# First six chunks decayed singly and converted weights placed late, in a kernel ordered by a planner

## The chip, the cores and the metric

The kernel runs on one core of a Trainium2 chip. The metric is device time in microseconds (us) of one execution. TensorE (PE) does the matrix products and transposes, VectorE (DVE), ScalarE (ACT) and GpSimd (POOL) the rest, and SyncE (SP) issues all transfers between DRAM and SBUF; each engine takes its own instructions strictly in order, and waits on semaphores for the others.

## The reference, cut to what matters

Linear attention with a decay per feature, then a soft mixture of eight experts over all tokens, then a gated layer. All data are float32; 4 batches of 768 tokens, 8 heads of 48.

```python
for t in range(S):
    state = alpha[:, :, t, :, None] * state + k_t v_t^T
    y[:, :, t] = q_t @ state
# y as x: 3072 tokens x 384
logits = x @ phi                      # 32 slots
slots = softmax over tokens(logits).T @ x
slots = relu(slots @ w1) @ w2         # per expert, 4 slots each
x = softmax over slots(logits) @ slots
out = (silu(xn @ w_gate) * (xn @ w_val)) @ w_out    # xn: x by its root mean square
```

## The kernel before

The 24 chunks of 128 tokens (6 per batch) go through attention one after the other. For chunk n the program has named operations. `sc n` makes the scores on PE (16 matmuls, line 509), `sb n` copies them out on ACT (L513), `sm n` sets the upper triangle to zero on POOL (L517). `kn n` turns the keys on PE (L496). `iv n` multiplies the scores with the values and the keys with the values (L530, L535), and `o n` adds what the old state gives (L543, L547). `sv n` writes the new state on DVE (L553), and `o n+1` waits for it. `x n` turns the result to token rows (L560). For a first chunk of a batch there is no old state, and `o n` stands for `iv n`.

Scores need decayed keys and queries. They are prepared for a *unit* of chunks at once (`units_of`): unit 0 is chunk 0, unit 1 chunks 1 and 2, and every further one three chunks. A unit of more than one chunk comes in two groups, two head pairs each, and a chunk can be scored only after both. For group x, `R x` is the running product of the decays (two scans on DVE, L449), `I x` its inverse (L457 and two scans, L458), `k x` the product of keys and inverse on DVE (L473), and `q x` that of queries and `R x` on POOL (L473 too; `BY_POOL` names the units for which POOL does it, here all nine). Rows come by SP (L431): decays into a ring of 2 places, keys and queries into rings of 5 places each. A place is taken again only after its last reader.

After every four chunks a softmax group follows (`gl`, `g1`, `gt`, `gd`, `s1`, `ga`, `s3`), and at the end `join` (`m1` to `mi`, where `siT` is made) starts the experts: `h` is the hidden layer (L749), `ht` its transpose (L760), `r` the second product (L770), eight of each; `sT` picks the slots. The expert weights are 64 loads of 384 KB (`w 1 ..`, `w 2 ..`; L734, L736), issued by SP all along the attention, each into one of 58 blocks of SBUF (`Q`). The gated layer then makes gates (`pg`, L902), and for each of 6 groups of 4 chunks and 12 slices of the feed-forward width the products `gv` (L1019), `sg`, `mu` (DVE, L1056), `hh`, `hl` (DVE, L1061) and `mm` (L1026 to L1028).

The weights of the gated layer arrive as 64-bit numbers and are converted in five steps (`wide_ops`): `cl` loads a piece (384 KB; L382), `ca` splits it on ACT (L385, L386), `cb` clamps on DVE (L389, L390), `cc` adds on POOL (L394), and `cd` writes the result on DVE (L397). `cl` takes the block of the raw numbers and also the block that `cd` will write into; `ca` takes a third one for its parts. 15 pieces (`g` for gate and value, `o` for the output weights) are loaded before the gated layer.

Nothing of the order is written by hand. Every operation is given to a `Plan` with an engine, an estimated cost, a priority, its predecessors and the places it takes and frees. `Plan.times` plays this through once when the program is built: at each step it takes, over all engines, the operation that could start first, but an engine may leave out one that is ready for one of lower priority number that becomes ready soon (`SOON`, `WAIT`, `LONG`, `LATE`, `CRIT`). The sequence that results is the order in which instructions are issued. Warm-up transposes (`wu`, L1089, four each, number `WARM`) have the last priority: they stand where PE had, by the plan, nothing else.

Of the kernel before, what the change touches and what calls it, by code (L numbers as in the profile page):

```python
# [16 lines left out]
P = 128  # L17
# [6 lines left out]
class Plan:  # L24
# [57 lines left out]
    def times(self):  # L82
# [29 lines left out]
        while ready:  # L112
# [24 lines left out]
            for e, b in best.items():  # L137
                x = min(b)
                wait = SOON if x[1] < LATE else WAIT if x[1] < CRIT else LONG
                c.append(min((y for y in b if y is x or y[0] <= x[0] + wait and y[1] < CRIT), key=lambda y: (y[1], y[2])) if wait else x)  # L140
# [36 lines left out]
BY_POOL = [("q", u) for u in range(9)]  # L177
WARM = 6
# [8 lines left out]
OHOLD = ("hl", 0, 0)  # L187
# [3 lines left out]
LD, KD_, SD_ = 0.8, 1.4, 1.4  # L191
XD, GD, CK = 3.366, 1.917, -7.005
AHEAD, BACK = 4, 4
EX0, EX_AT, EX_BY = 1, 4, 0.4
XA, XB, XC, GB1 = 195.8, 197.2, 197.4, 0.5
# [23 lines left out]
def network(tc, q, k, v, al, phi, w1, w2, wg, wv, wo, rg, aP, kP, qP, vP, phP, out):  # L219
# [33 lines left out]
    V.tensor_tensor(fold[:, 0, :], ident[:, 0:32], ident[:, 32:64], ALU.add)  # L253
    V.tensor_tensor(fold[:, 0, :], fold[:, 0, :], ident[:, 64:96], ALU.add)
    V.tensor_tensor(fold[:, 0, :], fold[:, 0, :], ident[:, 96:128], ALU.add)
    for g in range(1, 4):
        V.tensor_copy(fold[:, g, :], fold[:, 0, :])
# [113 lines left out]
    def wide_ops(plan, key, dst, w, prio, after, hold, new, use):  # L371
# [29 lines left out]
        plan.op(nm("cl"), "SP", 1130, prio[0], load, after, new=[cv, lim, *new], use=use)  # L401
# [260 lines left out]
    def join(plan, prio):  # L662
# [17 lines left out]
        plan.op("m1", "PE", 110, prio, lambda: T.transpose(plan("kn", "m1")[0:1, 0:P], m0, ident), [("g1", g)], new=[("kn", "m1")])  # L680
# [28 lines left out]
    def experts(plan, after, prio, n0=None):  # L709
# [142 lines left out]
    def gated(plan, prio):  # L852
# [25 lines left out]
        for i, key in enumerate(rest):  # L878
# [9 lines left out]
            w = ("Q", ("wf", f))  # L888
# [197 lines left out]

    def warm(bank, n):
# [11 lines left out]
    for u, (c0, j, groups) in enumerate(units):  # L1099
        for g, (p0, n) in enumerate(groups):  # L1100
            x, w = (u, g), n * j * C
            t = c0 - j + j * g / len(groups) - LD if u else -10
            for i, nm in enumerate("akq"):
                plan.op(("l", nm, x), "SP", 1.45 * w, t - 2 + 0.1 * i, lambda nm=nm, x=x: load_nat(nm, *x), last.get(nm, []), new=[(RING[nm], x)])
# [4 lines left out]
            for nm in "kq":  # L1109
                e, en, cost = (G, "Pool", 2.6 * w) if (nm, u) in BY_POOL else (V, "DVE", 60 + 1.3 * w)  # L1110
# [5 lines left out]
    for n in range(NCH):  # L1116
# [173 lines left out]
```

## Time and profile before

| | us |
|---|---|
| three runs, median (lowest to highest) | 405.32 (400.57 to 405.67) |
| the profiled execution | 403.42 |
| its span, from the first to the last instruction | 401.6 |
| PE, DVE, ACT, POOL busy in the span | 374.9, 299.0, 216.8, 122.6 |
| last chunk's product with the state (`o 23`) begins | 144.17 |
| first matmul of the experts | 152.15 |
| last pieces of the experts' second product (`r 1 3`) | 179.08 to 182.2 |
| first `mm` of the gated layer | 194.63 |
| last addition of the result on DVE | 394.75 |

The execution is 1.8 us longer than its span. The 1.9 us between it and the median are less than the spread of the three runs.

### The profile page before, as it was taken

How to read it: one execution, taken by the hardware profiler on the slowest of the kernel's cores; microseconds unless marked ns; L12 is line 12 of the kernel's file. 1: busy time of each engine (PE TensorE's matmuls, PEld its weight loads, DVE VectorE, ACT ScalarE, POOL GpSimd, SP SyncE). 2: the span in 40 equal slices, each digit the busy share in tenths (PEclk: the TensorE clock that was granted, in tenths of full speed). 3: DMA queues.
4: the chain of work that ended last, by engine and by line, in shares of the span. 5: the costliest groups of instructions: out<-in, count | busy, mean ns of one | idle time of the engine just before them, and what ended most of it. 6: DMA issues, size and time to landing. Idle time of an engine off the chain costs nothing.

```text
span 401.6 us, 8927 instructions
## 1 busy us (share of the span) xinstructions
PE 374.9 (93%) x3427; PEld 316.1 (79%) x3427; DVE 299.0 (74%) x563; ACT 216.8 (54%) x469; POOL 122.6 (31%) x150
## 2 busy tenths in 40 slices
PE   7689979998899999999889999999999999999993
PEld 6578858785777865436578999979899999999992
DVE  7999979879898557615989987769855667657652
ACT  2336535666574847311676786858856444444440
POOL 3445452635665415600155523243400000000000
PEclk9769989999999999999969999999999999999997
DMA  7899998996989679993021323213000102102012
GB/s 270 282 330 316 333 347 297 341 373 255 341 266 341 204 229 342 346 325 113 2 78 43 116 78 114 85 41 118 0 2 0 53 27 81 55 24 81 32 48 87
DMA packets 29252, 68.43 MB, mean 170 GB/s; under 512 B 3600, under 2 KB 9872, under 8 KB 29200
## 3 DMA queue, kind: packets, MB, share of 16 engines
q1 hardware_dynamic: 29200, 67.77, 48.7%
q8 instruction: 29, 0.48, 0.5%
q14 instruction: 23, 0.19, 0.1%
HBM read 63.04 MB, written 4.72 MB: 169 GB/s over the span
## 4 chain that ended last, share of the span: by engine, by line
PE 64%; DVE 16%; DMA 12%; issue 3%; ACT 2%; POOL 1%; SPq 0%; DVEq 0%; POOLq 0%; ACTq 0%
PE pstr L1019 4%; PE pssc L1019 4%; PE psmisc L1026 3%; PE pskn L1028 3%; PE psmisc L1028 3%; PE psy L1026 3%; PE psmisc L1027 3%; PE psU L1026 3%; PE pssc L509 3%; PE psy L1028 3%; PE psy L1027 3%; PE psU L1028 3%; PE psU L1027 3%; PE pskn L1026 3%; PE psy L530 3%
## 5 line engine op out<-in xcount | busy, mean ns | idle before, releaser
L1061 DVE TENSOR_TENSOR b<-b,b 128x512 fp32r<-128x512 f32 (+1 forms) x73 | 50.7, 697 | 26.3 <-PE psmisc L1027 10.1
L394 POOL TENSOR_TENSOR b<-b 128x384 int32<-128x384 int32 x36 | 40.5, 1126 | 96.5 <-DVE b L390 40.4
L1058 ACT CAST b<-b 128x512 fp32r<-128x512 f32 (+1 forms) x73 | 44.8, 617 | 36.6 <-DVE b L1056 34.5
L1056 DVE TENSOR_TENSOR b<-b,pssc 128x512 f32<-128x512 f32 (+1 forms) x73 | 49.2, 677 | 15.4 <-ACT b L1054 15.0
L1054 ACT ACTIVATE b<-pstr 128x512 f32<-128x512 f32 (+1 forms) x73 | 43.0, 594 | 24.2 <-PE pstr L1019 21.8
L517 POOL TENSOR_SCALAR_AFFINE_SELECT b<-b 128x512 f32<-128x512 f32 x48 | 32.2, 690 | 35.0 <-ACT b L513 34.9
L473 POOL TENSOR_TENSOR b<-b,b 128x768 f32<-128x768 f32 (+1 forms) x17 | 28.9, 1705 | 26.6 <-DVE pstr L457 12.2
L530 PE MATMUL psy<-b,b 128*48 128x128 f32 x384 | 29.7, 295 | 5.2 <-POOL b L517 4.3
L513 ACT COPY b<-pssc 128x512 f32<-128x512 f32 x48 | 26.7, 592 | 12.6 <-PE pssc L509 12.5
L458 DVE TENSOR_TENSOR_SCAN b<-b,pstr 128x387 f32<-128x387 f32 (+1 forms) x34 | 31.0, 912 | 1.7
L449 DVE TENSOR_TENSOR_SCAN b<-b,pstr 128x387 f32<-128x387 f32 (+1 forms) x34 | 29.0, 894 | 3.5 <-DMA b<-in_alpha_rows_dram 3.5
L509 PE MATMUL pssc<-b,b 48*128 48x128 f32 x384 | 30.1, 294 | 1.6 <-ACT b L513 1.2
L397 DVE SCALAR_TENSOR_TENSOR b<-b,b 128x384 int32<-128x384 int32 x36 | 27.2, 764 | 5.8 <-POOL b L394 5.8
L1019 PE MATMUL pssc<-y,b 128*128 128x512 f32 (+1 forms) x73 | 29.3, 401 | 2.1 <-DVE b L1056 1.7
L509 PEld LDWEIGHTS pssc<-b,b 48*128 48x128 f32 x384 | 24.8, 194 | 7.6 <-issue 4.9
L530 PEld LDWEIGHTS psy<-b,b 128*48 128x48 f32 x384 | 22.3, 131 | 10.5 <-POOL b L517 5.2
L1019 PE MATMUL pstr<-y,b 128*128 128x512 f32 (+1 forms) x73 | 29.4, 403 | 0.4 <-DVE b L906 0.4
L385 ACT ACTIVATE b<-b 128x384 f32<-128x384 f32 x36 | 20.8, 577 | 11.6 <-DMA b<-in_moe_w_val_dram 4.1
L1026 PE MATMUL pskn<-b,b 128*128 128x384 f32 x72 | 25.5, 354 | 0.2 <-ACT b L1058 0.2
L1028 PE MATMUL pskn<-b,b 128*128 128x384 f32 x72 | 24.9, 345 | 0.8 <-DVE b L1061 0.8
L1026 PE MATMUL psmisc<-b,b 128*128 128x384 f32 x72 | 24.7, 343 | 0.1
L1026 PE MATMUL psU<-b,b 128*128 128x384 f32 x72 | 24.6, 341 | 0.1
(226 smaller groups left out, 884.0 us busy)
## 6 DMA issues: line engine op xcount, KB each, us to landing
b<-in_moe_w_dram SPq DMA_DIRECT2D x64, 384.0 KB, 5.8
b<-in_alpha_rows_dram SPq DMA_DIRECT2D x14, 387.5 KB, 5.6
b<-in_k_rows_dram SPq DMA_DIRECT2D x14, 384.0 KB, 5.0
b<-in_q_rows_dram SPq DMA_DIRECT2D x14, 384.0 KB, 5.6
b<-in_v_rows_dram SPq DMA_DIRECT2D x24, 192.0 KB, 5.2
b<-in_moe_w_gate_dram SPq DMA_DIRECT2D x12, 384.0 KB, 4.8
b<-in_moe_w_val_dram SPq DMA_DIRECT2D x12, 384.0 KB, 3.9
b<-in_moe_w_out_dram SPq DMA_DIRECT2D x12, 384.0 KB, 3.8
```

Source lines behind the costliest of these rows:

```text
L394: G.tensor_tensor(ui, ui, r(), ALU.add)
L509: T.matmul(heads(plan(*sc_of(n)[a]))[:, p, :], kq("Tk", n, p)[r], kq("Tq", n, p)[r], start=True, stop=True)
L517: G.affine_select(s, s, pattern=[[0, NP], [1, C]], compare_op=ALU.is_ge, fill=0.0, base=0, channel_multiplier=-1)
L530: T.matmul(y[64 * a:64 * a + D, p, :], vv[:, h], heads(plan("scS", (n, a)))[:, p, :], start=p == 0, stop=first and p == NP - 1)
L1019: T.matmul(plan(r, ("gv", j, f))[:, s], G4(f // 3, a)[:, f % 3 * P:(f % 3 + 1) * P], plan("c4a", j)[:, s].bitcast(F32R), start=True, stop= ...
L1026: T.matmul(po, h, wo_of(f)[:, 0, :], start=(f % HALF == 0), stop=False)
L1027: T.matmul(po, h, wo_of(f)[:, 1, :], start=False, stop=False)
L1028: T.matmul(po, l, wo_of(f)[:, 0, :], start=False, stop=(f % HALF == HALF - 1))
L1054: plan.op(part("sg"), "ACT", 176 + 416 / np, pg, lambda g=g, SG=SG, s=s: A.activation(SG()[:, s], plan(*g)[:, s], AF.Silu), [part("gv"), * ...
L1056: plan.op(part("mu"), "DVE", 130 + 546 / np, pg, lambda val=val, SG=SG, s=s: V.tensor_tensor(SG()[:, s], SG()[:, s], plan(*val)[:, s], ALU ...
L1058: plan.op(part("hh"), "ACT", 194 + 422 / np, pg, lambda SG=SG, HH=HH, s=s: A.copy(HH()[:, s], SG()[:, s]), [part("mu"), *pre("hh")], new=n ...
L1061: lambda SG=SG, HH=HH, HL=HL, s=s: V.tensor_tensor(HL()[:, s], SG()[:, s], HH()[:, s], ALU.subtract), [part("hh"), *pre("hl")], new=new(hl),
```

## The change

There are nine edits in one.

1. `units_of`: the first six chunks are units of their own, with all four head pairs in one group. `BY_POOL` is widened to all units of the new count.
2. The priority of `sv n` is n - 1 in place of n, that of the rows and decays of the single chunks is set by `U1`, `U2`.
3. The matrix `fold`, the sum of four blocks of the identity, is made by POOL as an operation `fo` after `sm 4`, and not by DVE at the start.
4. `WARM` is 26 in place of 6.
5. `cl` no longer takes the block that is written into: for `g` pieces `cd` takes it, for `o` pieces `cd` writes into the block of the parts.
6. The pieces `o 3` to `o 5` may be converted once `sT 1` is done (`OHOLD`), before that after the first `hl`.
7. The second part of the root mean square (`sq`, `rm` to `rs`) has a later priority (`XB`, `XC`).
8. Expert weights are spread further in priority (`EX_BY`).
9. An engine may wait for a more urgent operation at least as long as the one ready would take; some estimated costs are changed.

```diff
-                wait = SOON if x[1] < LATE else WAIT if x[1] < CRIT else LONG
+                wait = SOON if x[1] < LATE else WAIT if x[1] < CRIT else max(LONG, ops[x[3]][1])
...
-BY_POOL = [("q", u) for u in range(9)]
-WARM = 6
+BY_POOL = [("q", u) for u in range(24)]
+WARM = 26
...
-OHOLD = ("hl", 0, 0)
+OHOLD = ("sT", 1)
...
+U1, U2, SV = -3, 0.8, 1
+SINGLE = 6
...
-EX0, EX_AT, EX_BY = 1, 4, 0.4
-XA, XB, XC, GB1 = 195.8, 197.2, 197.4, 0.5
+EX0, EX_AT, EX_BY = 1, 4, 0.6
+XA, XB, XC, GB1 = 195.8, 198.2, 199.4, 0.5
...
-    u = [(0, 1), (1, 2), (3, 3)] + [(c, 3) for c in range(6, chunks, 3)]
+    u = [(c, 1) for c in range(SINGLE)] + [(c, 3) for c in range(SINGLE, chunks, 3)]
...
-    V.tensor_tensor(fold[:, 0, :], ident[:, 0:32], ident[:, 32:64], ALU.add)
-    V.tensor_tensor(fold[:, 0, :], fold[:, 0, :], ident[:, 64:96], ALU.add)
-    V.tensor_tensor(fold[:, 0, :], fold[:, 0, :], ident[:, 96:128], ALU.add)
-    for g in range(1, 4):
-        V.tensor_copy(fold[:, g, :], fold[:, 0, :])
...
-        plan.op(nm("cl"), "SP", 1130, prio[0], load, after, new=[cv, lim, *new], use=use)
+        plan.op(nm("cl"), "SP", 1190, prio[0], load, after, new=[cv, lim])
...
-        plan.op(nm("cd"), "DVE", 650, prio[1], sign, [nm("cc")], use=[cv, cx, lim, *new, *use])
+        first = [("cd", (*key[:3], 0))] if key[0] == "g" and key[3] else []
+        plan.op(nm("cd"), "DVE", 650, prio[1], sign, [nm("cc"), *first], new=new, use=[cv, cx, lim, *use])
+    wf_of = lambda f: ("Q", ("cx", ("o", f)) if wide else ("wf", f))
...
+    def folds():
+        for i in range(1, 4):
+            G.tensor_tensor(fold[:, 0, :], fold[:, 0, :] if i > 1 else ident[:, 0:32], ident[:, 32 * i:32 * i + 32], ALU.add)
+        G.tensor_copy(fold[:, 1:4, :], fold[:, 0:1, :].to_broadcast([P, 3, NS]))
...
-            t = c0 - j + j * g / len(groups) - LD if u else -10
+            t = -10 if not u else U1 + U2 * u if j == 1 else c0 - j + j * g / len(groups) - LD
...
-            plan.op(("sv", n), "DVE", 350, n, lambda n=n: state(n), [("o", n), *[("ck", (u, g)) for g in gs]], use=[("U", n), ("gm", u)])
+            plan.op(("sv", n), "DVE", 350, n - SV, lambda n=n: state(n), [("o", n), *[("ck", (u, g)) for g in gs]], use=[("U", n), ("gm", u)])
...
+    plan.op("fo", "Pool", 900, AHEAD, folds, [("sm", AHEAD, 1)])
```

What it does to the order is seen at three places. The first is PE at the start, up to what follows the scores of chunk 0 (`pskn` holds turned keys, `pssc` scores, `psy` the result of a chunk, `psmisc` is the bank of the warm-up transposes). Before:

```order
L1089 MATMUL psmisc_70<-ident 128x128 x24
L496 MATMUL pskn_67<-ident,b_97 128x128 x4
L509 MATMUL pssc_65<-b_102,b_97 128x128
L509 MATMUL pssc_66<-b_102,b_97 128x128
...
L530 MATMUL psy_69<-b_114,b_118 48x128
L530 MATMUL psy_69<-b_115,b_118 48x128
...
L535 MATMUL psU_68<-b_118 48x48 x8
L496 MATMUL pskn_67<-ident,b_98 128x128 x2
```

The same place in the changed kernel, up to the scores of chunk 1:

```order
L1095 MATMUL psmisc_70<-ident 128x128 x28
L497 MATMUL pskn_67<-ident,b_91 128x128 x4
L510 MATMUL pssc_65<-b_96,b_91 128x128
L510 MATMUL pssc_66<-b_96,b_91 128x128
...
L1095 MATMUL psmisc_70<-ident 128x128 x20
L497 MATMUL pskn_67<-ident,b_92 128x128 x4
L510 MATMUL pssc_65<-b_97,b_92 128x128
L510 MATMUL pssc_66<-b_97,b_92 128x128
```

All 24 warm-up transposes stood at the very start; now 28 stand there, 20 between the scores of chunk 0 and the keys of chunk 1 (whose scores now come ahead of chunk 0's product with the values), 4 before the scores of chunk 2, 8 between `o 3` and `iv 4`, 16 around `join` and before `r 1 3`, and 28 behind the last `mm`.

The second place is DVE from the keys of the second group on (`b_98`, `b_99`, `b_100` are keys, `psU` the sum for the state). Before:

```order
L473 TENSOR_TENSOR b_98<-b_98,b_113 128x512
L253 TENSOR_TENSOR fold<-ident 128x32
L254 TENSOR_TENSOR fold<-fold,ident 128x32
L255 TENSOR_TENSOR fold<-fold,ident 128x32
L257 COPY fold<-fold 128x32 x3
L449 SCALAR_TENSOR_TENSOR b_111<-b_107,pstr_63 128x258 x2
...
L473 TENSOR_TENSOR b_99<-b_99,b_112 128x512
L449 SCALAR_TENSOR_TENSOR b_109<-b_108,pstr_63 128x387 x2
...
L473 TENSOR_TENSOR b_100<-b_100,b_113 128x768
L553 TENSOR_TENSOR b_115<-psU_68,b_114 128x192
```

The same stretch of the changed kernel (`b_92` to `b_94` are the keys of chunks 1 to 3):

```order
L474 TENSOR_TENSOR b_92<-b_92,b_107 128x512
L450 SCALAR_TENSOR_TENSOR b_105<-b_101,pstr_63 128x258 x2
...
L474 TENSOR_TENSOR b_93<-b_93,b_106 128x512
L554 TENSOR_TENSOR b_109<-psU_68,b_108 128x192
L450 SCALAR_TENSOR_TENSOR b_103<-b_102,pstr_63 128x258 x2
...
L474 TENSOR_TENSOR b_94<-b_94,b_107 128x512
L450 SCALAR_TENSOR_TENSOR b_104<-b_102,pstr_63 128x258 x2
L554 TENSOR_TENSOR b_108<-psU_68,b_108 128x192
```

The six instructions of `fold` are gone, each key product now completes a chunk, and the first state step (`sv 0`) stands behind the keys of chunk 2, where those of chunks 1 and 2 and a half of 3 to 5 stood ahead of it.

The third place is DVE at the start of the gated layer, from the last `hl` of the first slice to that of the second one (`cN` and `ss` belong to the root mean square; L389, L390 and L397 before are L386, L387 and L394 after). Before:

```order
L1061 TENSOR_TENSOR b_2374<-b_2360,b_2371 128x256
L990 SCALAR_TENSOR_TENSOR cN<-cN,rr 128x640
L906 TENSOR_TENSOR b_2357<-pstr_64,b_2357 64x384
L389 TENSOR_SCALAR b_2390<-b_2390 128x384
L390 TENSOR_SCALAR b_2390<-b_2390 128x384
L906 TENSOR_TENSOR b_2357<-pssc_65,b_2357 64x384
L389 TENSOR_SCALAR b_2400<-b_2400 128x384
L390 TENSOR_SCALAR b_2400<-b_2400 128x384
L397 SCALAR_TENSOR_TENSOR b_2257<-b_2256,b_2390 128x384
L1056 TENSOR_TENSOR b_2409<-b_2409,pssc_66 128x512
L397 SCALAR_TENSOR_TENSOR b_2261<-b_2260,b_2400 128x384
L1061 TENSOR_TENSOR b_2436<-b_2409,b_2428 128x512
```

The same stretch of the changed kernel:

```order
L1062 TENSOR_TENSOR b_2442<-b_2426,b_2437 128x256
L965 TENSOR_TENSOR b_2428<-psmisc_70,cN 128x128
L1057 TENSOR_TENSOR b_2452<-b_2452,pssc_66 128x512
L892 TENSOR_TENSOR b_2462<-b_2366,b_2462 128x384
L907 TENSOR_TENSOR b_2431<-pssc_65,b_2431 64x384
L1062 TENSOR_TENSOR b_2472<-b_2452,b_2469 128x512
```

Ten instructions between the two became four; the conversions of `o 3` and `o 4` moved ahead of the first `hl`, and the root mean square from there to behind the second one.

## Rows read from the trace of the kernel before

**Rows 1.** Busy us of each engine in a stretch; then PEclk, DMA share, GB/s.

```profile
10.00:20.00 10.00, 6.86 (x58) 5.33 (x58) 9.45 (x22) 3.07 (x10) 4.79 (x5) 0.72 0.83 282
```

**Rows 2.** Stretches of 4 us, with the same columns.

```profile
96.00:100.00 4.00, 2.77 (x35) 1.66 (x32) 3.90 (x9) 3.15 (x8) 1.65 (x3) 1.00 0.42 122
160.00:164.00 4.00, 4.00 (x58) 1.68 (x54) 3.46 (x7) 1.32 (x3) 2.65 (x3) 1.00 1.00 359
```

**Rows 3.** Tile `ident` up to 10 us: ns of one, minimum, median, maximum.

```profile
L1089 PEld LDWEIGHTS psmisc<-ident x24: 183/230/230, 1.5 to 6.3; 128*128 128x128 f32 x24
...
L496 PEld LDWEIGHTS pskn<-ident,b x4: 140/142/143, 7.9 to 8.2; 128*128 128x128 f32 x4
```

**Rows 4.** Timeline of PE: start, duration, instruction, idle time before it and its end.

```profile
21.47 2.07 PE L509 MATMUL pssc<-b,b 48*128 48x128 f32 x14 [1.24 <-ACT b L513]
...
33.71 1.16 PE L509 MATMUL pssc<-b,b 48*128 48x128 f32 x16
...
38.09 1.16 PE L509 MATMUL pssc<-b,b 48*128 48x128 f32 x16
...
55.93 1.73 PE L530 MATMUL psy<-b,b 128*48 128x128 f32 x13 [2.59 <-POOL b L517]
...
60.94 1.16 PE L509 MATMUL pssc<-b,b 48*128 48x128 f32 x16
...
125.40 0.71 PE L509 MATMUL pssc<-b,b 48*128 48x128 f32 x8
```

**Rows 5.** Timeline of DVE in attention; the last row is a stretch of the softmax tile.

```profile
7.80 1.26 DVE L449 TENSOR_TENSOR_SCAN b<-b,pstr 128x258 f32<-128x258 f32 x2
...
11.47 0.61 DVE L253 TENSOR_TENSOR fold<-ident 128x32 f32<-128x32 f32 x1
...
12.84 1.27 DVE L449 TENSOR_TENSOR_SCAN b<-b,pstr 128x258 f32<-128x258 f32 x2
...
27.30 1.79 DVE L449 TENSOR_TENSOR_SCAN b<-b,pstr 128x387 f32<-128x387 f32 x2
...
32.76 1.80 DVE L449 TENSOR_TENSOR_SCAN b<-b,pstr 128x387 f32<-128x387 f32 x2
...
48.00 0.95 DVE L473 TENSOR_TENSOR b<-b,b 128x768 f32<-128x768 f32 x1
...
60.03 0.36 DVE L553 TENSOR_TENSOR b<-psU,b 128x192 f32<-128x192 f32 x1 [2.71 <-PE psU L547]
...
122.84 0.95 DVE L473 TENSOR_TENSOR b<-b,b 128x768 f32<-128x768 f32 x1
...
47.00:57.00 10.00, 1.29 (x10) 0.36 (x10) 2.18 (x9) 1.30 (x5) 0.92 1.02 378
```

**Rows 6.** Timelines of SP and POOL: a load of queries and its product.

```profile
46.76 0.80 SPq L431 DMA_DIRECT2D b<-in_q_rows_dram  x2
...
53.65 1.63 POOL L473 TENSOR_TENSOR b<-b,b 128x768 f32<-128x768 f32 x1 [3.73 <-DVE pstr L457]
```

**Rows 7.** Timeline of PE from the last chunk to the end of the experts.

```profile
144.17 1.08 PE L543 MATMUL psy<-b,b 48*48 48x128 f32 x16
...
152.15 2.80 PE L749 MATMUL pssc<-b,siT 128*32 128x256 f32 x48 [0.35 <-DVE siT L692]
...
167.76 1.47 PE L770 MATMUL pskn<-b,x 128*32 128x384 f32 x16
...
179.08 3.14 PE L770 MATMUL pskn<-b,x 128*32 128x384 f32 x16
...
182.15 0.87 PE L1089 MATMUL psy<-ident 128*128 128x128 f32 x6
```

**Rows 8.** Timeline of DVE at the start of the gated layer, and its last addition.

```profile
196.29 0.82 DVE L990 SCALAR_TENSOR_TENSOR cN<-cN,rr 128x640 f32<-128x640 f32 x1
...
202.96 0.68 DVE L1061 TENSOR_TENSOR b<-b,b 128x512 fp32r<-128x512 f32 x1
...
209.88 0.68 DVE L1061 TENSOR_TENSOR b<-b,b 128x512 fp32r<-128x512 f32 x1
...
394.75 0.56 DVE L1077 TENSOR_TENSOR b<-psmisc,b 128x384 f32<-128x384 f32 x1
```

More of the change, by code (lines that the diff above doesn't have):

```diff
@@ L412, in piece @@
         else:
-            t, w, m, at = ("Q", ("wf", key[1])), wo[key[1] * P:(key[1] + 1) * P], 0, 0
+            t, w, m, at = wf_of(key[1]), wo[key[1] * P:(key[1] + 1) * P], 0, 0
         dst = lambda: plan(*t)[:, at:at + CW]
-        new, use = ([], [t]) if m else ([t], [])
+        new, use = ([], [t]) if m else ([] if wide and key[0] == "o" else [t], [])
         if wide:
@@ L678, in m9 @@
                 T.matmul(plan("kn", "m9")[:, kk * NS:(kk + 1) * NS], acc[:, kk * P:(kk + 1) * P], foldS, start=True, stop=True)
-        plan.op("m1", "PE", 110, prio, lambda: T.transpose(plan("kn", "m1")[0:1, 0:P], m0, ident), [("g1", g)], new=[("kn", "m1")])
+        plan.op("m1", "PE", 110, prio, lambda: T.transpose(plan("kn", "m1")[0:1, 0:P], m0, ident), [("g1", g), *[x for x in ["fo"] if x in plan.ops]], new=[("kn", "m1")])
         plan.op("m2", "DVE", 450, prio, m2, ["m1"], use=[("kn", "m1")])
@@ L739, in experts @@
         for i, x in enumerate(seq):
-            plan.op(("w", *x), "SP", 1130, EX_AT + i * EX_BY, lambda x=x: load(*x), [("w", *seq[i - 1])] if i else after,
+            plan.op(("w", *x), "SP", 1190, EX_AT + i * EX_BY, lambda x=x: load(*x), [("w", *seq[i - 1])] if i else after,
                     new=[("Q", (f"w{x[0]}", *x[1:]))])
@@ L887, in gated @@
                 continue
-            w = ("Q", ("wf", f))
+            w = wf_of(f)
             plan.op(("hi", f), "ACT", 510, po, lambda f=f, w=w: A.copy(wo_of(f)[:, 0, :], plan(*w)[:, 0:DM]), [("cd", key), *(["mi"] if f else [])], new=[("Q", ("wo", f))], use=[w])
@@ L1101, in network @@
             x, w = (u, g), n * j * C
-            t = c0 - j + j * g / len(groups) - LD if u else -10
+            t = -10 if not u else U1 + U2 * u if j == 1 else c0 - j + j * g / len(groups) - LD
             for i, nm in enumerate("akq"):
-                plan.op(("l", nm, x), "SP", 1.45 * w, t - 2 + 0.1 * i, lambda nm=nm, x=x: load_nat(nm, *x), last.get(nm, []), new=[(RING[nm], x)])
+                plan.op(("l", nm, x), "SP", 1.52 * w, t - 2 + 0.1 * i, lambda nm=nm, x=x: load_nat(nm, *x), last.get(nm, []), new=[(RING[nm], x)])
                 last[nm] = [("l", nm, x)]
@@ L1109, in network @@
             for nm in "kq":
-                e, en, cost = (G, "Pool", 2.6 * w) if (nm, u) in BY_POOL else (V, "DVE", 60 + 1.3 * w)
+                e, en, cost = (G, "Pool", 2.35 * w) if (nm, u) in BY_POOL else (V, "DVE", 60 + 1.45 * w)
                 plan.op((nm, x), en, cost, t, lambda nm=nm, x=x, e=e: prep_m(nm, *x, e), [("l", nm, x), ("R" if nm == "q" else "I", x)],
```

## Prediction

> **What bounds the kernel now.** I read the stretches first, then the timelines of PE and DVE side by side. The time table gives PE 374.9 of 401.6 us, 93%, so whatever shortens the run must close gaps or slow stretches of PE. There are three places with such loss. At the start DVE works without a pause and PE waits for it: in 10 to 20 us DVE is busy 9.45 of 10, PE 6.86, at a granted clock of 0.72 [rows 1], and 14 score matmuls take 2.07 us at 21.5, where 16 take 1.16 at 33.7 [rows 4], that is 148 ns each against 72: the lower of the two clock levels, 1.2 GHz in place of 2.4. In the experts DMA ends the waits: the last product, 16 matmuls, lasts 3.14 us where its kind needs 1.47 [rows 7]. At the start of the gated layer DVE again: the second `mm` needs an `hl` that DVE begins only at 202.96 [rows 8], 8.3 us after the first `mm`. I take the rest, the other 70 slices, to cost the same in either kernel.
>
> **The start, part by part.** DVE first. A group of 512 columns (two scans, the inverse, the keys) lasts 11.47 - 7.80 = 3.67 us, and `fold` 12.84 - 11.47 = 1.37 [rows 5]. A group of 768 lasts 32.76 - 27.30 = 5.46, of which one state step is 0.26, so 5.2 [rows 5]. Six chunks singly cost 6 x 3.67 = 22.0, plus 0.5 where the first key product runs beside POOL; in units of 1, 2 and 3 chunks they cost 3 x 3.67 + 2 x 5.2 = 21.4. So single chunks cost DVE 0.6 us and `fold` gives back 1.4; the keys of chunk 5 come at 3.7 + 22.5 + two state steps and a wait of about 0.5, some 27.3, as before (27.3, the start of the next group [rows 5]). DVE gains next to nothing. What changes is PE: chunk 1 can be scored at 11.5 and not after both groups of unit 1 (12.84 + 3.67 = 16.5), chunk 3 at 3.66 + 4 x 3.67 + 0.5 + 0.3 = 19.1 and not at 27.3, where PE had to begin three chunks at once.
>
> PE needs 38.09 - 33.71 = 4.4 us per chunk at the full clock [rows 4], DVE 4.0 with the state step, so PE trails DVE by one chunk through the first six. I walked both queues. `o 0` ends near 15.8 (20 transposes of 0.145 us stand ahead of it: six last 0.87 [rows 7]), while DVE reaches `sv 0` at 15.3: it stands 0.5 to 0.7 there, and with it `R 3` and all decays behind. `sv 1` to `sv 4` find their products done. Two groups more of 5.2 with three state steps put chunks 6 to 8 at 38.9, hardly later than before (32.76 + 5.46 = 38.2), and two more, now with the first softmax on DVE as well (2.2 us here, the softmax tile's row [rows 5]), put chunk 9 at about 53.4, 1.9 us of it for state steps, waits and products slowed beside POOL. PE has finished `kn 8` by 50.4 and begins `sc 9` at 53.4. Before, it began at 60.94 [rows 4], though its keys were ready at 48.95 [rows 5]: POOL stood 3.73 us at the queries of a later group, with `sm 7` queued behind them, because these were loaded only at 46.76, when chunk 5 had given its place in the ring free [rows 6]; PE then waited 2.59 for POOL [rows 4], and DVE 2.71 for PE's state [rows 5]. With one place per single chunk the same queries wait for chunk 4, which by the same walk ends 11 us sooner. **The gain at chunk 9 is 60.94 - 53.4 = 7.5 us.**
>
> That it lasts to the end of attention is not given. At PE's own pace `o 23` begins at 144.17 - 7.5 [rows 7]. DVE must bring the keys of the last unit in time. Before, from the keys of chunk 9 (48.95) to those (122.84 + 0.95 = 123.8) it took 74.8 us [rows 5]. The changed order has in this stretch two conversions less (three instructions of 384 columns; by the 0.68 of 512 columns [rows 8] 0.5 each, 3.0 in all) and a softmax group less (2.2); the stop of 2.71 for PE's state [rows 5] falls away, since PE is then ahead. That leaves 66.9, and 53.4 + 66.9 = 120.3. PE began these scores at 125.40 [rows 4], and wants them at 117.9: 2.4 lost if DVE had no other wait in the 66.9, nothing if it had 2.4 of waits on PE, which come earlier with PE. I take 0.5.
>
> **Transposes and clock.** The 28 at the start end near 7.9, when the first keys come, so they cost nothing. The 20 fill a gap ahead of chunk 1 in which PE stood idle. Row by row: while PE did nothing but 24 transposes, its weight loads took 230 ns; right behind them, with no other matmul in between, they took 142 [rows 3]. So here transposes alone raised it. The Trainium skill ("TensorE: Matmul & The Clock Gate", Part 4: PE-mode transpose) says that transposes don't count as work in this way and don't bring the full clock. Rows 3 speak against that; what would follow from it is rival B. The 16 around `join` cost 0 in its waits and 8 x 0.145 = 1.2 ahead of `r 1 3` if its weights are there. The 28 at the end can start once the last addition is done, at 394.75 + 0.56 = 395.3 [rows 8]; 28 x 0.145 are 4.1, and the span goes on to 401.6, 6.3 later, for the output's transfer, so 0, at most 1; I take 0.2.
>
> **`fold` on POOL** has no row: DVE did it in 1.37, and where DVE needs 0.95 for 768 columns POOL needs 1.63 [rows 5, 6]; at that ratio 2.4. But POOL does it in four instructions and not six, so 1 to 2.4; I take 1.5. Behind it queue the queries of unit 6 and `sm 5`; both wait for DVE or PE beyond that, so 0, and 1.5 at the other bound, for `iv 5` alone.
>
> **Blocks and DMA.** The `cl` pieces took two blocks per `g` pair and one per `o` more. When these ran out, SP stood with all rows behind it: in 96 to 100 DMA moved 122 GB/s, against 359 when fed [rows 2]. By the order, SP now meets its first block to wait for only when all keys are issued. Behind the first expert layer's first product 19 loads are left, where there were 21; one load of 0.393 MB at 359 GB/s is 1.1 us, so the DMA-bound end comes 2.2 nearer to `mi`. DMA must, however, keep up with a PE that is 7 us ahead. Up to there 60 such loads and 24 chunks of 0.985 MB, by the shapes of the loads, are 47.2 MB; at 359 GB/s 132 us, at nine tenths of it 146. PE gets there, the middle of `h 0 0`, at 152.15 + 1.4 - 7 = 146.6 [rows 7]. Of that I count 1.5 us lost: the experts gain 2.2, less 1.2 for the transposes, less 1.5.
>
> `cd` now takes a block when it runs: `cd g200` waits for the `mm` of three slices earlier in DVE's queue, with two `mu` behind it. `hl` is then two slices (5 us) ahead of PE, and the wait is at most one slice of 2.1; 0, with 2 for the range.
>
> **The gated start.** From `rs` at 196.29 + 0.82 = 197.1 to 202.96 DVE did ten instructions of other work and then `hl`, which ended at 203.64 [rows 8]. The changed order has four: the conversions of `o 3` and `o 4` stand among the first root mean square and the gates, where DVE has waits, and the long root mean square behind the second `hl`. With the first `hl` at the same place (ended about 196.4, ahead of L990), four instructions of 0.2 to 0.69 and `hl` itself (0.68) are 2.9: that `hl` ends at 199.3, 4.3 us earlier. The two `hl` behind it come at about 203.6 and 207.9, where the second of them ended at 209.88 + 0.68 = 210.6 [rows 8], since the 2.7 us of the root mean square lie there now. So gain 2.7 to 4.3, less 0 to 1 if `o 3` lands late, as `cb` stands ahead of `sq 0`; I take 3.0.
>
> **The sum.** 403.42 - 7.5 + 0.5 (attention) - 2.2 + 1.2 + 1.5 (experts) - 3.0 (gated start) + 0.2 (end) = 394.1. The median of the runs lies 1.9 above the profiled one, their lowest 2.9 below, so I leave it there: **394**. Bounds: with all gains whole and nothing lost, 403.4 - 7.5 - 2.2 - 4.3 = 389.4; with 2.4 lost on DVE and 4 to DMA 394.1 + 1.9 + 2.5 = 398.5, and with 2 at `cd g200` on top 400.5.
>
> **Rivals.** *A: DMA eats the lead.* The weights come no sooner than 2.2 us ahead of today, and PE waits in the experts. For it speaks that the last `r` waits for its weights now [rows 7] with PE late, and so more with PE early; against it the stretches at 122 GB/s, which were a want of blocks [rows 2]. 403.4 - 1 - 3 + 0.2 = 399.6. *B: the clock falls in the first 28 us.* PE's chunk then costs up to 8.8 us (twice 4.4), and `sv 0` to `sv 3`, which now stand ahead of the next decays in DVE's queue, hold these up: it decides as soon as a chunk on PE takes longer than the 4.0 us of DVE. Four chunks at 7.4 to 8.8 less 4.0 are 13.6 to 19 us on DVE; from 53.4, chunk 9 is at 67 and 6 us later than before: 403.4 + 6 - 3 + 0.2 = 406.6, slower. This is what the skill's rule would give. *C: the gated start doesn't gain,* because ACT converts `o 3` to `o 5` ahead of the first gates and their loads land late: 397. *D: more,* since from chunk 9's scores to `o 23` PE took 144.17 - 60.94 = 83.2 us [rows 4, 7], where 14.5 chunks of 4.4 are 64, and what lies between isn't all softmax products: if 6 us of waits on POOL and DVE go there too, 388.
>
> **How the numbers follow.** Forecast 0.52, A 0.20, B 0.08, C 0.10, D 0.10. 387.5 to 401 leaves out B and a piece of each of A and D. Two per cent are 8 us, 395.3, which is about what a measurement of this kernel can tell from no change: below it lie four fifths of the forecast and D, 0.52; above 411 almost nothing of B, yet something unseen may: 0.07; the rest is 0.41.
>
> **What would show it.** Right: `sc 9` near 53, a clock near 1.0 from 8 to 28, DVE busy to 50; `o 23` near 137; `r 1 3` under 2 us; the second `mm` near 199. Wrong: DVE standing at L554 in the first 30 us (B), `r` products of 2 to 3 us from 165 on (A), `cb` waiting near 177 (C).

## The result and the profile after

The changed kernel takes 388.25 us (median of four runs, 385.04 to 389.34) against 404.98 (400.57 to 405.67): a ratio of 0.9596, with an interval of 0.9507 to 0.9685 (this and all ratios leave out executions more than 1.5% above the fastest of their kernel). The profiled execution takes 389.34 us, its span 387.6; before they were 403.42 and 401.6. So 14.1 us went, where 9.4 were forecast.

The stretches first (us busy of PE, PEld, DVE, ACT, POOL, then granted clock, DMA share, GB/s). The first row is the start of the changed kernel, the second all of it up to the end of the experts:

```profile
8.00:28.00 20.00, 19.09 (x268) 16.46 (x268) 19.04 (x38) 10.19 (x26) 11.96 (x14) 1.00 0.93 300
...
0.00:170.68 170.68, 160.74 (x2338) 122.85 (x2339) 143.98 (x280) 92.72 (x235) 83.89 (x116) 1.00 0.93 327
```

The same stretch of the kernel before, up to its end of the experts:

```profile
0.00:182.22 182.22, 166.28 (x2286) 124.65 (x2287) 143.74 (x279) 91.89 (x233) 83.69 (x111) 0.95 0.88 307
```

The clock no longer falls at the start (1.00, where [rows 1] show 0.72). 327 GB/s for 170.68 us are 55.8 MB, 307 for 182.22 are 55.9: by the end of the experts the program has loaded the same bytes, and now 11.5 us sooner.

PE's timeline in the changed kernel (start, duration) at the places of [rows 4, 7]: the scores of chunk 9, `o 23`, the first expert product, the last one, the first `mm`:

```profile
52.34 1.30 PE L510 MATMUL pssc<-b,b 48*128 48x128 f32 x16
...
134.52 1.08 PE L544 MATMUL psy<-b,b 48*48 48x128 f32 x16
...
142.89 2.80 PE L750 MATMUL pssc<-b,siT 128*32 128x256 f32 x48
...
168.53 2.15 PE L771 MATMUL pskn<-b,x 128*32 128x384 f32 x16
...
183.74 0.34 PE L1027 MATMUL pskn<-b,b 128*128 128x384 f32 x1
```

The timelines of SP and POOL there answer to [rows 6]: the load of the queries for which POOL stood 3.73 us is issued at 35.91, where it was 46.76; POOL masks chunks 7 and 8 and then multiplies these queries without a wait.

```profile
35.91 0.33 SPq L432 DMA_DIRECT2D b<-in_q_rows_dram  x1
...
44.34 2.00 POOL L518 TENSOR_SCALAR_AFFINE_SELECT b<-b 128x512 f32<-128x512 f32 x2
47.77 1.23 POOL L518 TENSOR_SCALAR_AFFINE_SELECT b<-b 128x512 f32<-128x512 f32 x2 [1.44 <-ACT b L514]
49.05 1.64 POOL L474 TENSOR_TENSOR b<-b,b 128x768 f32<-128x768 f32 x1
```

DVE's timeline at the last keys of chunk 9's unit, at the second `hl` of the gated layer and at the last addition, as [rows 5, 8]. Those keys end at 52.82, and chunk 9's scores begin at 52.34 with the first group's: DVE sets chunk 9 now. The `hl` ends at 187.13, 3.4 us behind the first `mm`, where it was 9.0.

```profile
51.88 0.94 DVE L474 TENSOR_TENSOR b<-b,b 128x768 f32<-128x768 f32 x1
...
186.44 0.69 DVE L1062 TENSOR_TENSOR b<-b,b 128x512 fp32r<-128x512 f32 x1
...
380.30 0.56 DVE L1078 TENSOR_TENSOR b<-psmisc,b 128x384 f32<-128x384 f32 x1
```

Between these marks the 14.1 us divide so:

| stretch | before | after | difference | forecast |
|---|---|---|---|---|
| start to the scores of chunk 9 | 60.94 | 52.34 | -8.6 | -7.5 |
| from there to `o 23` | 83.23 | 82.18 | -1.0 | +0.5 |
| `o 23` to the end of the experts | 38.05 | 36.16 | -1.9 | +0.5 |
| from there to the first `mm` | 12.41 | 13.06 | +0.7 | 0 |
| first `mm` to the last addition | 200.12 | 196.56 | -3.6 | -3.0 |
| from there to the end of the execution | 8.67 | 9.04 | +0.4 | +0.2 |

Only the 0.7 ahead of the first `mm` was not in the sum at all. What the table cannot say is which edit made which row; the experiments ask that.

### The profile page after: what moved, and what is told of

Same layout as the page of the kernel before. It is cut to its first block, busy times and chain, and to the rows that moved or that the text cites. A ratio compares the mean times of both kernels' runs of the same rounds, so it can differ in the third digit from the quotient of the medians.

```text
span 387.6 us, 9101 instructions
## 1 busy us (share of the span) xinstructions
PE 371.3 (96%) x3507; PEld 316.9 (82%) x3507; DVE 297.4 (77%) x564; ACT 216.6 (56%) x471; POOL 122.4 (32%) x155
## 4 chain that ended last, share of the span: by engine, by line
PE 75%; DVE 18%; issue 3%; DMA 2%; ACT 1%; DVEq 0%; SPq 0%; ACTq 0%
PE pstr L1020 4%; PE pssc L510 4%; PE pssc L1020 4%; PE psy L531 3%; PE pskn L1029 3%; PE psy L1027 3%; PE psU L1027 3%; PE psmisc L1027 3%; PE psy L1029 3%; PE psmisc L1029 3%; PE psmisc L1028 3%; PE psy L1028 3%; PE psU L1029 3%; PE psU L1028 3%; PE pskn L1027 3%
## 5 line engine op out<-in xcount | busy, mean ns | idle before, releaser
L1062 DVE TENSOR_TENSOR b<-b,b 128x512 fp32r<-128x512 f32 (+1 forms) x73 | 50.0, 687 | 30.0 <-ACT b L1059 10.9
L518 POOL TENSOR_SCALAR_AFFINE_SELECT b<-b 128x512 f32<-128x512 f32 x48 | 33.2, 715 | 29.7 <-ACT b L514 29.5
L474 POOL TENSOR_TENSOR b<-b,b 128x768 f32<-128x768 f32 (+1 forms) x18 | 27.0, 1502 | 19.8 <-DVE pstr L458 8.5
L510 PE MATMUL pssc<-b,b 48*128 48x128 f32 x384 | 28.3, 285 | 1.1 <-ACT x L564 1.0
L510 PEld LDWEIGHTS pssc<-b,b 48*128 48x128 f32 x384 | 23.7, 187 | 6.1 <-issue 4.9
L394 DVE SCALAR_TENSOR_TENSOR b<-b,b 128x384 int32<-128x384 int32 x36 | 25.7, 726 | 3.7 <-POOL b L391 3.6
L531 PE MATMUL psy<-b,b 128*48 128x128 f32 x384 | 25.9, 277 | 0.1
L1027 PE MATMUL psy<-b,b 128*128 128x384 f32 x72 | 24.6, 341 | 0.0
## 6 DMA issues: line engine op xcount, KB each, us to landing
b<-in_alpha_rows_dram SPq DMA_DIRECT2D x12, 387.5 KB, 5.4
```

The source lines that it names most:

```text
L510: T.matmul(heads(plan(*sc_of(n)[a]))[:, p, :], kq("Tk", n, p)[r], kq("Tq", n, p)[r], start=True, stop=True)
L518: G.affine_select(s, s, pattern=[[0, NP], [1, C]], compare_op=ALU.is_ge, fill=0.0, base=0, channel_multiplier=-1)
L531: T.matmul(y[64 * a:64 * a + D, p, :], vv[:, h], heads(plan("scS", (n, a)))[:, p, :], start=p == 0, stop=first and p == NP - 1)
L1027: T.matmul(po, h, wo_of(f)[:, 0, :], start=(f % HALF == 0), stop=False)
L1062: lambda SG=SG, HH=HH, HL=HL, s=s: V.tensor_tensor(HL()[:, s], SG()[:, s], HH()[:, s], ALU.subtract), [part("hh"), *pre("hl")], new=new(hl),
```

## The experiments

Edits to the changed kernel leave all its other edits in place. Where an edit changes what the plan sees, the whole order is planned anew; in e1, e5 (against e2) and e12 only transposes are left out and the order stays word for word. Times are medians; the ratio, with its 95% interval, is to the kernel before on the same chip, whose medians were 403.4 to 404.6.

| run | time | ratio (interval) | chunk 9 | `o 23` | end of experts |
|---|---|---|---|---|---|
| before (profiled) | 404.98 | | 60.94 | 144.17 | 182.22 |
| after | 388.25 | 0.9596 (0.9507 to 0.9685) | 52.34 | 134.52 | 170.68 |
| e1 no start transposes | 389.01 | 0.9611 (0.9532 to 0.969) | 52.25 | 134.28 | 172.89 |
| e2 old units | 389.04 | 0.9611 (0.953 to 0.9691) | 53.31 | 139.36 | 175.60 |
| e3 single chunks alone | 405.36 | 1.0043 (1.0003 to 1.0082) | 54.51 | 136.31 | 181.05 |
| e4 old gated start | 391.52 | 0.9666 (0.9585 to 0.9748) | 51.61 | 135.13 | 171.82 |
| e5 old units, quiet | 389.24 | 0.9631 (0.9542 to 0.972) | 54.23 | 134.56 | 171.99 |
| e6 `cl` takes blocks | 390.23 | 0.9685 (0.9616 to 0.9755) | 51.69 | 133.24 | 172.70 |
| e7 late blocks alone | 401.03 | 0.9968 (0.992 to 1.0015) | 58.50 | 142.51 | 178.87 |
| e8 single and late blocks | 397.40 | 0.9841 (0.9775 to 0.9908) | 57.36 | 140.79 | 176.66 |
| e9 old spread and costs | 394.53 | 0.9734 (0.966 to 0.9808) | 51.67 | 136.24 | 172.36 |
| e10 spread and costs alone | 402.58 | 0.9985 (0.9944 to 1.0026) | 56.37 | 143.89 | 183.62 |
| e11 costs alone | 396.75 | 0.9795 (0.9718 to 0.9872) | 55.95 | 138.11 | 176.24 |
| e12 no late transposes | 389.81 | 0.9666 (0.9611 to 0.9721) | 51.84 | 133.27 | 170.83 |

The last three columns are from one profiled execution each, read off PE's timeline; e3's is the lowest of its ten, e2's the highest of its five. The scores of chunk 0 begin at 7.98 to 8.92 us in these, latest in the changed kernel, so chunk 9 is better counted from there: 52.42 us before, 43.42 after, 9.0 less. Against the changed kernel the times of e1, e2, e4, e5, e6, e9 and e12 can be compared by medians or by the two ratios, which differ by up to 1.6 us.

**e1: the start without its transposes.** In the changed kernel:

```diff
-plan.op(("wu", i), "PE", 436, 1e6, lambda i=i: warm(plan("misc", ("wu", i)), 4), ...
+plan.op(("wu", i), "PE", 436, 1e6, lambda i=i: warm(plan("misc", ("wu", i)), 0 if 7 <= i < 15 else 4), ...
```

> The changed kernel with the 32 transposes left out that stand between the scores of chunk 0 and chunk 4's values; every other instruction in the same order. Theory (the lead comes from the order, single chunks let PE begin early): the scores of chunk 9 begin at 52.3 to 53.5, the time is 389 to 391. Rival (the lead comes from the clock that the transposes keep up): the granted clock in 8 to 28 us falls towards 0.7, a chunk on PE takes up to 8.8 us, DVE stands at the first state steps, the scores of chunk 9 begin at 58 or later, the time is 395 to 401.

The clock did fall, but briefly. Stretches of e1, from the one in which PE stood:

```profile
10.00:12.00 2.00, 0.78 (x8) 0.65 (x10) 1.97 (x4) 0.59 (x3) 1.61 (x2) 1.00 0.95 324
12.00:16.00 4.00, 4.00 (x54) 3.79 (x54) 3.17 (x8) 1.86 (x6) 2.87 (x3) 0.62 0.91 275
16.00:20.00 4.00, 4.00 (x70) 3.56 (x68) 3.79 (x8) 2.33 (x7) 2.37 (x3) 0.95 1.02 331
```

The first two of them in the changed kernel, where 20 transposes fill the gap:

```profile
10.00:12.00 2.00, 2.00 (x20) 1.99 (x19) 1.90 (x5) 1.31 (x4) 2.00 (x3) 1.00 0.89 311
12.00:16.00 4.00, 3.89 (x60) 3.32 (x59) 3.79 (x9) 1.85 (x6) 3.00 (x4) 1.00 0.94 304
```

DVE's timeline in e1 has one stop of PE's making between 8 and 28 us, at `sv 0`, and behind it one for decay rows:

```profile
15.44 0.36 DVE L554 TENSOR_TENSOR b<-psU,b 128x192 f32<-128x192 f32 x1 [0.62 <-PE psU L536]
...
28.66 1.81 DVE L450 TENSOR_TENSOR_SCAN b<-b,pstr 128x387 f32<-128x387 f32 x2 [0.75 <-DMA b<-in_alpha_rows_dram]
```

The stop is made up: `sv 3` stands at 27.56, where e4, e6 and e12, which have the transposes and the same order there, have 27.55 to 27.78. So with single chunks PE has enough slack beside DVE to spend some four us at a low clock. Chunk 9 comes at 52.25; counted from the scores of chunk 0 that is 0.7 us later than in the changed kernel, with the wait for rows in between, and whether this wait has to do with the clock isn't shown. The theory's numbers came, the rival's did not.

**e2: the old units in the changed kernel.**

```diff
-    u = [(c, 1) for c in range(SINGLE)] + [(c, 3) for c in range(SINGLE, chunks, 3)]
+    u = [(0, 1), (1, 2), (3, 3)] + [(c, 3) for c in range(6, chunks, 3)]
```

> The changed kernel with the old units (1, 2, 3 chunks and then threes), all other edits kept; 64 transposes now lie in the first gaps of PE. Theory: the scores of chunk 9 begin at 59 to 61 as before the change, though the clock stays up, and the time is 396 to 399. Rival: with the clock up PE catches up, the scores of chunk 9 begin at 53 to 55, the time is 390 to 391.

The theory missed: chunk 9 at 53.3 and 389.0 us, 0.8 above the changed kernel, within the scatter of both. The rival's chunk 9 came, with a time 1 us under its own, and so e1 and e2 together left a choice: either of the two is enough, or neither is needed.

**e5: neither.** The order of e2, its 64 transposes in PE's first gaps left out:

```diff
-lambda i=i: warm(plan("misc", ("wu", i)), 4)
+lambda i=i: warm(plan("misc", ("wu", i)), 0 if 7 <= i < 23 else 4)
```

> As e2_old_units (the changed kernel with the old units) in the same order, with the 64 transposes left out that lay in PE's first gaps. Theory (either is enough by itself: single chunks start PE early, or transposes keep its clock so that it catches up): with neither the scores of chunk 9 begin at 58 to 61 and the time is 394 to 398. Rival (the other edits to the order and the blocks make the gain in attention): the scores of chunk 9 begin at 53 to 55, the time is 388 to 391.

389.24 us, the rival's range: neither is needed. Without single chunks and without transposes chunk 9 still comes at 54.2 and `o 23` at 134.6. POOL's timeline shows what is not as before:

```profile
47.05 1.30 POOL L518 TENSOR_SCALAR_AFFINE_SELECT b<-b 128x512 f32<-128x512 f32 x2 [2.56 <-ACT b L514]
49.31 1.64 POOL L474 TENSOR_TENSOR b<-b,b 128x768 f32<-128x768 f32 x1 [0.96 <-DMA b<-in_q_rows_dram]
```

Both masks of chunk 7 stand ahead of the queries that POOL waited for. By e11, below, the estimated costs are enough to put them there; that no other edit would, with the old units, wasn't tried.

**e3: single chunks alone, on the kernel before.**

```diff
-    u = [(0, 1), (1, 2), (3, 3)] + [(c, 3) for c in range(6, chunks, 3)]
+    u = [(c, 1) for c in range(6)] + [(c, 3) for c in range(6, chunks, 3)]
-plan.op(("sv", n), "DVE", 350, n, ...
+plan.op(("sv", n), "DVE", 350, n - 1, ...
```

> The kernel before with the first six chunks as units of their own and the state step's priority n - 1, no other edit, so no transposes beyond the 24 at the start. Theory: the scores of chunk 9 begin at 53 to 56, and the time is 395 to 398 (of 14 us gained, some 8). Rival: without the transposes the clock falls and DVE stands at the state steps, the scores of chunk 9 begin at 58 to 61, the time is 401 to 406.

Half of the theory came: chunk 9 at 54.5, `o 23` at 136.3, 7.9 us earlier. The queries that POOL had stood for are issued at 38.35, and it takes them without a wait. The time didn't come: 405.36, no gain. The rival's range holds that number, but not for the rival's reason: DVE doesn't wait for PE at any state step up to 45 us. From `o 23` to the first expert product it takes 13.1 us where it took 8.0. DVE and PE there, each from its timeline:

```profile
141.20 1.33 DVE L397 SCALAR_TENSOR_TENSOR b<-b,b 128x384 int32<-128x384 int32 x1 [0.89 <-POOL b L394]
...
143.04 0.27 PE L680 MATMUL pskn<-ident,sm 128*1 128x128 f32 x1 [2.06 <-DVE sm L589]
...
149.41 4.34 PE L749 MATMUL pssc<-b,siT 128*32 128x256 f32 x48 [0.35 <-DVE siT L692]
```

Conversions of weights stand ahead of the small steps of `join` on DVE; PE waits, its clock falls, and 48 matmuls take 4.34 us where they took 2.80 [rows 7]. The stretches show the clock, and what DMA brought from `o 23` to the experts' end:

```profile
148.00:152.00 4.00, 3.65 (x33) 2.14 (x37) 1.67 (x7) 1.79 (x3) 1.04 (x9) 0.50 0.41 156
...
136.31:181.05 44.74, 39.09 (x433) 19.23 (x433) 23.28 (x54) 18.23 (x44) 14.79 (x28) 0.92 0.86 291
```

The outcome is that of the prediction's rival A, in a kernel other than the one it was set up for: the lead is there and is eaten behind attention, and the last expert product lasts 3.16 us, waiting for its weights (3.14 before [rows 7]). But of the 6.7 us that e3 takes longer from `o 23` to the experts' end, 5.1 lie ahead of the first expert product, where PE waits for DVE and not for DMA. Which of the two would have ended the experts alone isn't shown.

**e11: the changed cost estimates alone, on the kernel before.**

```diff
-plan.op(("w", *x), "SP", 1130, ...          # cl: 1130 too
+plan.op(("w", *x), "SP", 1190, ...
-plan.op(("l", nm, x), "SP", 1.45 * w, ...
+plan.op(("l", nm, x), "SP", 1.52 * w, ...
-(G, "Pool", 2.6 * w) if (nm, u) in BY_POOL else (V, "DVE", 60 + 1.3 * w)
+(G, "Pool", 2.35 * w) if (nm, u) in BY_POOL else (V, "DVE", 60 + 1.45 * w)
```

> The kernel before with the new estimated costs alone. Their one effect near chunk 9 is that POOL masks the second half of chunk 7 ahead of the queries of unit 4, where it stood 3.73 us. Theory (this stop of POOL is the loss at chunk 9): the scores of chunk 9 begin at 54 to 57, the time is 396 to 400. Rival (the spread of the expert loads is what counts): the scores of chunk 9 begin at 59 to 61, the time is 401 to 405.

The theory's numbers came: 396.75 us, a ratio of 0.9795, and chunk 9 at 55.95, from an edit that changes no instruction, only five estimates. POOL's timeline, and PE's at `iv 7`, which had waited 2.59 us for POOL [rows 4]:

```profile
49.36 1.25 POOL L517 TENSOR_SCALAR_AFFINE_SELECT b<-b 128x512 f32<-128x512 f32 x1 [0.33 <-ACT b L513]
52.74 1.64 POOL L473 TENSOR_TENSOR b<-b,b 128x768 f32<-128x768 f32 x1 [2.13 <-DMA b<-in_q_rows_dram]
...
52.22 1.08 PE L530 MATMUL psy<-b,b 128*48 128x128 f32 x16
```

POOL still waits for the queries, 2.13 us, but the second mask of chunk 7 is done before, and `iv 7` no longer stands behind it. This isn't the one effect near chunk 9, as the expectation had it: small steps of the first softmax group moved on DVE and PE as well, and loads of values on SP. So that the two instructions on POOL make the whole 5.0 us is read from the waits, not tried alone.

**e10 and e9: the spread of the expert loads.** e10 adds it to e11; e9 takes both out of the changed kernel.

```diff
-EX0, EX_AT, EX_BY = 1, 4, 0.4
+EX0, EX_AT, EX_BY = 1, 4, 0.6
```

> The kernel before with the new spread of the expert loads (0.6) and the new estimated costs, no other edit. Theory: the scores of chunk 9 begin at 54 to 57, o 23 at 135 to 139, the time is 392 to 397, most of the gain without single chunks, transposes, late blocks and the new gated start. Rival: these two do nothing without the others, the time is 400 to 405.

> The changed kernel with the old spread of the expert loads (0.4) and the old estimated costs of loads and key and query products; single chunks, transposes, late blocks and the new gated start kept. Theory (these two edits to the planner's numbers, not the single chunks, give most of what attention and experts gained, since they decide how many weights SP has ahead of rows and where POOL's masks stand): 393 to 397. Rival (single chunks, transposes and blocks together are enough): 388 to 390.5.

e10 missed: chunk 9 at 56.4 as in e11, but the lead was gone at `o 23` (143.9), and the time is 402.58, in the rival's range. A stretch in which it went, in e10 and then in e11:

```profile
80.00:100.00 20.00, 17.18 (x278) 13.77 (x274) 19.45 (x36) 12.52 (x33) 10.64 (x11) 1.00 0.88 303
```

```profile
80.00:100.00 20.00, 19.00 (x292) 14.97 (x291) 15.87 (x31) 12.59 (x32) 10.79 (x12) 1.00 0.92 341
```

DVE is the busy one in e10 (19.45 of 20), and PE has lost 1.8 us more. In the changed kernel the two edits belong to the gain: e9 came within the theory's range, 394.53, 6.3 us above it (5.6 by the ratios). Its loss isn't at chunk 9, which comes at 51.67 with the old estimates: there single chunks, with the other edits, are enough. Why the spread costs 5.8 us beside costs alone, and whether it costs or gains beside the rest, these runs don't settle: in the changed kernel the two were only taken out together.

**e7, e8 and e6: the late blocks** alone, with single chunks, and taken out of the changed kernel. As added:

```diff
-plan.op(nm("cl"), "SP", 1130, prio[0], load, after, new=[cv, lim, *new], use=use)
+plan.op(nm("cl"), "SP", 1130, prio[0], load, after, new=[cv, lim])
...
-plan.op(nm("cd"), "DVE", 650, prio[1], sign, [nm("cc")], use=[cv, cx, lim, *new, *use])
+plan.op(nm("cd"), "DVE", 650, prio[1], sign, [nm("cc"), *first], new=new, use=[cv, cx, lim, *use])
```

> The kernel before with the later taking of blocks as its only edit. Theory: attention as before (o 23 at 143 to 145), the experts end 2 to 4 us earlier, the time is 399 to 402. Rival (SP, no longer held up, brings the rows of attention earlier as well): o 23 at 137 to 140, the time is 394 to 398.

> The kernel before with single chunks (and the state step's priority n - 1) and the later taking of blocks, no other edit. Theory: the two need each other: o 23 at 135 to 137, the experts end at 172 to 175, the time is 394 to 397, though single chunks alone gave nothing. Rival: the loss of single chunks lies at the join and not with the blocks, the time is 401 to 405.

> The changed kernel in which the load of a raw piece again takes the block that will be written into, all other edits kept. Theory (single chunks alone gained 8 us in attention and lost them in the experts to DMA; later taking of blocks is what lets the weights come early enough): o 23 begins at 134 to 137, the experts end at 175 to 180 and not at 170.7, the time is 394 to 399. Rival (the spread of the expert loads or the transposes at the join pass the lead on): the experts end at 170 to 173, the time is 388 to 391.

Alone they are worth 2.4 us by the medians (401.03, the theory's range), 1.3 by the ratio, and the interval (0.992 to 1.0015) reaches no change. With single chunks all three forecasts were missed, by little in the time: 397.4 for 394 to 397, `o 23` at 140.8, the experts' end at 176.7. But that is 8 us below e3, and from `o 23` to the experts' end e8 needs 35.9 us where e3 needed 44.7; so the late blocks do keep the lead of single chunks from being lost there. In front of it e8 is slower than e3, chunk 9 at 57.4: PE stood 2.70 us for DVE and then ran at the lower clock (0.75 in 28 to 40), and DVE in turn stood at a state step, on its timeline:

```profile
37.24 0.36 DVE L556 TENSOR_TENSOR b<-psU,b 128x192 f32<-128x192 f32 x1 [2.25 <-PE psU L550]
```

Out of the changed kernel they cost 2.0 us by the medians and 3.6 by the ratios, and the theory of e6 (394 and more) fell: the rival's range came, and with the other edits most of the lead comes through without them. From `o 23` to the experts' end e6 takes 39.5 us, 3.3 more than the changed kernel; its chain of waits (start, us, what) has there:

```profile
160.51 6.15 DMA b<-in_moe_w_dram
```

**e4: the old gated start.**

```diff
-OHOLD = ("sT", 1)
+OHOLD = ("hl", 0, 0)
-XA, XB, XC, GB1 = 195.8, 198.2, 199.4, 0.5
+XA, XB, XC, GB1 = 195.8, 197.2, 197.4, 0.5
```

> The changed kernel with the old place of the conversions of o 3 to o 5 and of the second root mean square; order up to the experts' end unchanged. Theory: from the first mm to the second hl it takes 9.0 as before and not 3.4, PE waits there, the time is 392 to 393.5. Rival (the gated start is shorter because the experts end earlier and the loads are there): as the changed kernel, 388 to 390.

391.52, just under the theory's 392 and above the rival's 390: 3.3 above the changed kernel by the medians, 2.8 by the ratios, and its four executions lie above all four of that. PE and DVE in e4, each from its timeline, beside the second `hl`:

```profile
191.22 0.50 PE L1020 MATMUL pssc<-y,b 128*128 128x512 f32 x1 [1.73 <-DVE b L1057]
...
192.61 0.68 DVE L1062 TENSOR_TENSOR b<-b,b 128x512 fp32r<-128x512 f32 x1
```

It ends at 193.29, 8.1 behind the first `mm` (185.23), and the wait on DVE is back. This part of the change stands by itself; its two edits, 6 and 7, were not tried apart.

**e12: no late transposes** (`0 if i >= 15 else 4`).

> The changed kernel, same order, with the 44 late transposes left out: 16 around the join and before r 1 3, 28 behind the last mm. Theory (those at the join lie in waits and cost nothing, 8 cost 1.0 ahead of r 1 3 if its weights are there, those at the end 0 to 0.5): 387 to 388.3. Rival (they keep the clock up through the join and the gated start, or r 1 3 waits for DMA anyway and nothing changes): 388.3 to 391.

389.81: no gain, the rival's range. What the 16 transposes stand in for is seen on PE's timeline: the last expert product begins 2.05 us earlier than with them, lasts 4.35 in place of 2.15, and ends at the same time (170.83, before 170.68).

```profile
166.48 4.35 PE L771 MATMUL pskn<-b,x 128*32 128x384 f32 x16
```

The chain of waits says what it stood for:

```profile
163.49 5.82 DMA b<-in_moe_w_dram
169.35 1.48 PE pskn L771 x10
170.83 0.80 PE psy L1095 x6
```

## Why the prediction was right, and where it was not

**The time.** 388.25 lies in the range (387.5 to 401.0), near its lower end, on the side that was forecast, and 5.7 below 394. Of these, the terms of the sum account for 4.7: chunk 9 1.1, the rest of attention 1.5, the experts 2.4, the gated start 0.6, less 0.9 behind the experts and at the end. The rest is the median, which lies 1.1 below the profiled execution. Rival D named 388, but by luck: it wanted 6 us more between the scores of chunk 9 and `o 23`, and that stretch became 1.0 shorter.

**What bound chunk 9** was right: POOL at the queries, with `sm 7` behind them, PE behind POOL. **What takes that away** was right as one of two ways, and taken for the only one. The ring did what was said: the queries that POOL stood for are issued 10.9 us sooner (35.91 for 46.76, where 11 were forecast), and DVE then sets chunk 9, with its keys at 52.82 for a forecast 53.4. Single chunks alone give 6.4 of the 8.6 us (e3), and with the old estimates in the changed kernel chunk 9 is as early (e9). But the prediction passed over the changed estimates without a price, and e11 gains 5.0 with them alone, e5 6.7 without single chunks. So both take the same stop away, and the second to come finds it gone: of the whole change, single chunks can be left out at no measurable loss (e2, e5), and alone they gain nothing in the end (e3). The changed kernel without both was not run.

**That the lead lasts** was put as rival A against the forecast (0.20 against 0.52). e3 shows that it need not last, the changed kernel that it does. The 1.5 us that the sum took off for DMA were not lost: DMA was busy 0.93 of the time to the experts' end, not 0.88. In all fourteen profiled executions 55.8 to 56.4 MB have come by then (mean GB/s times the end). That alone doesn't say that loads set the end, as any order has to bring these bytes by then. From `o 23` to that end it takes 35.9 to 36.4 us in e8, e9, e2, e7 and the changed kernel, and in the chains of waits of these (e7's doesn't reach so far back) no load of expert weights stands behind 155 us. In the nine others one does, and they take 36.7 (e4) to 44.7 (e3). Among them are the three in which `o 23` comes earlier than in the changed kernel: e12 with 37.6, e1 with 38.6, e6 with 39.5. So the changed kernel stands where PE's pace and the weights meet, and this may be why taking one edit out, or adding slack to attention, moves it so little; no run changes the loads alone.

**The transposes.** Rival B did not come: the clock is 1.00 from 8 to 28 us, and DVE has no stop there, not even the 0.5 to 0.7 that the prediction allowed at `sv 0`. That transposes hold the clock up is shown by e1 against the changed kernel, 0.62 against 1.00 in the same four us of the same order, and it speaks against the Trainium skill ("TensorE: Matmul & The Clock Gate", Part 4: PE-mode transpose) as [rows 3] did. The price that rival B put on a fall was too high in e1, where it lasted some four us and chunk 9 is at most 0.7 us later; its mechanism, DVE standing at a state step for a slow PE, is there in e1 for 0.62 us and in e8 for 2.25. The 1.2 us ahead of `r 1 3` were not paid, because its weights are what ends there (e12); that product still lasts 2.15 us, and not the under 2 that was given as a sign.

**The gated start** was right as worked out: 3.0 forecast, 3.6 by the marks, 2.8 to 3.3 by e4. The second `hl` comes 5.6 us earlier against the first `mm`, where 4.3 were forecast. By the fourth that lead is 3.8, since the root mean square now stands between. Rival C did not come: no `cb` waits on DVE from 170 to 240 us.

**`fold` and `cd g200`** cost nothing that shows. On POOL's timeline the four instructions of `fold` are 0.25, 0.58 for two and 0.27 in the changed kernel, 1.1 together (1.8 in e5), within the bounds; from 170 to 300 us `cd` waits on DVE for POOL only, at most 0.91 us. No run has `fold`, the spread of the loads or the rule for waiting (the first half of edit 9) as its only difference.

## What to carry to other kernels

A planner's estimates are part of the program: where an order is computed, a changed number is priced by the order that it makes, on every engine, and an edit that "only changes estimates" is the first to look at, not the last. Where several edits each remove the same stop, taking one away shows nothing at that stop; adding each alone to the kernel before, as e3 and e11 do, tells. A lead won early has to pass every later bound, here `join` on DVE and the loads of weights, before it is time saved.

## What the runs showed of the hardware

Float32 transposes alone held the granted clock at 1.00 in a stretch that fell to 0.62 without them, behind 2 us in which PE worked 0.78, with the other instructions the same (e1). The fall cost no time that can be told from the scatter, because DVE set the pace there. The clock also rose while PE did nothing but transposes: among the 28 at the start of the changed kernel (tile `ident` up to 8 us: ns of one, minimum, median, maximum) most weight loads take 231 ns, and the last ten 139 to 145. (The granted clock of that stretch reads 1.00 throughout, so the rise is read from the loads alone.)

```profile
L1095 PEld LDWEIGHTS psmisc<-ident x28: 139/231/231, 1.5 to 6.2; 128*128 128x128 f32 x28
```
